# An FFT convolution with a gated unit, forward and backward: spectra kept as separate real and imaginary tiles of two channel blocks, and the step back from them as two 64-row TensorE tiles

## The chip, the cores and the metric

The kernel runs on one NeuronCore of a Trainium2 chip. The metric is the device time of one execution, in microseconds (us). Before the change it is 535.45 us, the median of three runs (534.1 to 536.3).

## What is computed

Forward and all gradients of one block: a layer norm, a long convolution done with an FFT over the sequence (length S = 2048, padded to 4096, D = 512 channels), a gated unit of width F = 1376, and their product added to the input. Inputs and outputs are bfloat16.

```python
def _A_ref(q, k, v, shift_k, ssm_k, ssm_D):
    k_shift = sum of 4 shifted copies of k, each times a column of shift_k
    kv = k_shift * v
    kv_f = rfft(pad(kv, 2 * S)); kf_f = rfft(pad(ssm_k, 2 * S))
    y = irfft(kv_f * kf_f)[:S] + kv * ssm_D
    return q * y

def _B_ref(x, w_gate, w_up, w_down):
    g, u = x @ w_gate, x @ w_up
    return (sigmoid(g) * u) @ w_down

xn = layernorm(A_q)
out = A_q + _A_ref(xn, A_k, A_v, ...) * silu(_B_ref(xn, ...))
# returned: out, and the gradients of A_q, A_k, A_v, A_shift_k, A_ssm_k, A_ssm_D,
# B_w_gate, B_w_up, B_w_down for a given grad_out
```

## The kernel before

**The order.** The kernel does not issue instructions as it is written. Python generators ("streams") yield after each piece of work; `run_streams` takes the next piece from the stream that is furthest behind its share, a start and an end written beside each stream. Every operation goes into a record (`Rec.add`), with the operations it depends on. `Rec.order` then lays all of them out with a cost for each (`cost`, `dcost`) and a model of free PSUM banks, and `emit` (line 505) issues them in that order, so every instruction of the profile has line 505. Copies out of PSUM (`evac`) go to ScalarE or VectorE, as the layout decides. Each engine and each DMA queue then works in the order given.

**PSUM.** There are eight banks. `KINDS` names the slots: `mm2` is a pair of banks for 1024 f32 columns, `acc` (banks 4 and 5) and `tr` (6 and 7) single ones. In the forward stage `mm2` may use all four pairs; from the middle stage on `ps_mm` uses `mm2c`, two pairs.

**Stages.** Forward (`strF`, `strK`, `strV`, `strX` together): the gated unit; the spectrum of the filter; the product of shifted k and v; its spectrum, the product of spectra, and the way back to `y2A`. Middle (`stepB`, with the first pieces of `dW` and `frontC`): gradients through the gated unit. Back (`dW`, `frontC`, `backC`): the weights' gradients, whose operands come through DMA transposes on SP's queue; the spectrum of the gradient; and two ways back, one for the gradient of kv and one for that of the filter.

**The transform of 128 channels** (one group `cg` of four) has three steps. `step1`: 128 matmuls of 128 columns, each with 32 output partitions, four beside each other in the array (column tiles). `flip`: a transpose on VectorE for each block `qq`, a quarter of a group. `step3` (line 881): a matmul with the constant `BD`, 128 by 128, two of 512 columns for a block. Its result has the real part of the spectrum in partitions 0 to 63 and the imaginary part in 64 to 127. Back from a spectrum: `inv3` (line 888) with the spectrum as weights and a constant as moving operand, 8 times 2 matmuls of 128 columns for a block, the two of a pair summing in PSUM; then `inv1`.

**The product of two spectra** needs real with imaginary parts, which lie in other partitions. So `swap` (line 903) makes a second copy with the halves exchanged, by two VectorE copies of 64 partitions: of the filter's spectrum in `strK` (`KF`, `Ks`) and of the gradient's in `frontC` (`Xc`, `Xs`). VectorE multiplies twice per product, and the two results, with their signs in the constants `RS1`, `RS2`, `RC1`, `RC2`, are summed by `inv3`'s pair of matmuls. `strX` has one product for each block, `backC` two (line 1258). 16 blocks are worked through in each.

**KK_d**, in HBM, keeps both forward spectra of each block: `strK` and `strX` store them through POOL's queue (256 KB each), and `ld_KK` loads both of a block (512 KB) on SP's queue into one of three buffers; load n + 3 is recorded after the last `inv3` of block n (line 1267).

Of the kernel before, what the change touches and what calls it, by code (L numbers as in the profile page):

```python
# [16 lines left out]
P = 128  # L17
# [12 lines left out]
NKF = 3  # L30
# [112 lines left out]
class PTile:  # L143

    def __init__(self, kind):
        self.kind = kind
        self.bank = None
        self.left = 0
        self.last = 0.0

# [5 lines left out]
class Op:  # L156
    __slots__ = ("n", "alts", "deps", "succ", "wait", "ready", "dma", "tiles", "done", "fin", "eng", "soft")
# [12 lines left out]
class Rec:  # L170
# [5 lines left out]
    KINDS = {"mm2": [(0, 1), (2, 3), (4, 5), (6, 7)], "mm2c": [(0, 1), (2, 3)], "mm1": [(0,), (1,), (2,), (3,)],  # L176
             "acc": [(4,), (5,)], "tr": [(6,), (7,)]}

    def __init__(self, nc, tc, slab, psum):
        self.nc, self.tc, self.psum = nc, tc, psum  # L180
        self.slab_name = slab.name
        self.ops = []
        self.lastw, self.readers = {}, {}
        self.cache = {}
        self.narrow = False
        for e in self.ENGS:
            setattr(self, e, EngRec(self, e))
# [48 lines left out]
    def add(self, alts):  # L236
# [37 lines left out]
        op.dma = "dma" in meth  # L274
        self.ops.append(op)
# [7 lines left out]

    def cost(self, alt):
# [67 lines left out]
    def order(self):  # L352
# [3 lines left out]
        for op in ops:  # L356
            for v in op.tiles:
                group.setdefault(id(v), []).append(op)
# [44 lines left out]
        while ndone < len(ops):  # L403
            best = None
            for e in self.ENGS:
# [3 lines left out]
                if now[e]:  # L409
                    c = (free[e], now[e][0], e, 0)  # L410
                elif soon[e]:
                    c = (soon[e][0][0], soon[e][0][1], e, 0)
# [13 lines left out]
            if shared:  # L426
                either.remove(op)
            else:
                heapq.heappop(now[e] if now[e] else soon[e])
            q = 1 if shared and e == "vector" else 0  # L430
            new = [v for v in op.tiles if v.bank is None]
            if new:
                got = slot(new[0].kind)
                if got is None:
                    blocked[new[0].kind].append(op)
                    continue
                if got[0] > t:
                    op.ready = got[0]
                    push(op)
                    continue  # L440
                new[0].bank = got[1][0]
                for b in got[1]:
                    owner[b] = new[0]
            alt = op.alts[q]
# [90 lines left out]
class Consts:  # L535
# [27 lines left out]
    def small(self, negpi, TB, I32, after):  # L563
# [33 lines left out]
        an = tmp([5, 128], i32)  # L597
        nc.gpsimd.tensor_scalar(an[:, 0], pr[:, 0], pcf[:, 0:1], None, ALU.add)
        nc.gpsimd.tensor_scalar(an[:, 2], pr[:, 1], pcf[:, 0:1], pcf[:, 0:1], ALU.add, ALU.add)
        nc.gpsimd.tensor_scalar(an[:, 1], an[:, 2], 4.0, None, ALU.add)  # L600
        nc.gpsimd.tensor_scalar(an[:, 3], pr[:, 1], 4.0, None, ALU.add)
        nc.gpsimd.tensor_copy(an[:, 4], pr[:, 1])
        nc.vector.tensor_single_scalar(an, an, 15, ALU.bitwise_and)
        tri = tmp([5, 128], f32)
# [6 lines left out]
        nc.vector.tensor_tensor(TB[:, 1:5], tri[:, 1:5], mask[:, 1:2].to_broadcast([P, 4, 128]), ALU.mult)  # L611
# [11 lines left out]
def kernel_impl(ctx, tc, A_q, A_k, A_v, A_shift_k, A_ssm_k, A_ssm_D, B_x, B_w_gate, B_w_up, B_w_down,  # L623
# [8 lines left out]
    KK_d = dram.tile([NG, 4, 2, P, 1024], bf16, name="KK_d")  # L632
# [13 lines left out]
    def ps_mm(shape, dt=f32, name=None):  # L646
        return nc.ps(PS["mm"], shape, dt)
# [9 lines left out]
    TB = Ring(ar, [5, 128]).ap  # L657
    BD, RC2, RS1, RC1, RS2 = (TB[:, q] for q in (0, 1, 2, 4, 3))
# [187 lines left out]
    Ks_r, KF_r = Ring(ar, [1024], n=NKF), Ring(ar, [1024], n=NKF)  # L846
# [3 lines left out]
    Xc_r = Ring(ar, [1024], n=2)  # L850
# [26 lines left out]
    def step3(Qf, dst):  # L877
        ps = ps_mm([1024], name="ps_x")
        for h in range(2):
            nc.tensor.matmul(ps[:, h * 512:(h + 1) * 512], BD, Qf[:, 2 * h:2 * h + 2].rearrange("p a (k b) -> p a b k", b=2),  # L880
                             start=True, stop=True)
        nc.evac(dst, ps, 1024)

    def inv3(parts, qq, Bg):
        ps = ps_mm([8, NJ, 8], name="ps_b")
        for g in range(8):
            for n, (Y, Rt) in enumerate(parts):
                nc.tensor.matmul(ps[:, g].rearrange("p j x -> p (j x)"), Y[:, g * 128:(g + 1) * 128], Rt,
                                 start=(n == 0), stop=(n == len(parts) - 1))
        nc.evac(Bg[:, :, 8 * qq:8 * qq + 8].rearrange("p j g e c -> p g j (e c)"), ps[:], 1024)  # L890
# [12 lines left out]
    def swap(dst, src):  # L903
        nc.vector.tensor_copy(dst[0:64], src[64:128])
        nc.vector.tensor_copy(dst[64:128], src[0:64])
# [11 lines left out]
    def strK():  # L917
        for cg in range(NG):
# [15 lines left out]
            for qq in range(4):  # L934
                while stA["nX"] + NKF <= 4 * cg + qq:
                    yield 0
                Qf, KF, Ks = QfK_r.next(), KF_r.next(), Ks_r.next()
                flip(Qg, qq, Qf)
                yield 1024
                step3(Qf, KF)  # L940
                swap(Ks, KF)
                nc.gpsimd.dma_start(KK_d[cg, qq, 0], KF)
                stA["K", 4 * cg + qq] = (KF, Ks)
                yield 1024
# [30 lines left out]
    def strX():  # L975
        yield from gen_ci()
        for cg in range(NG):
            while ("QgV", cg) not in stA or ("K", 4 * cg) not in stA:
                yield 0
            Qg = stA.pop(("QgV", cg))  # L980
            Bg = Bg_r.next()
            xs = {}
            for qq in range(5):
                if qq < 4:
                    Qf, Xc = QfV_r.next(), Xc_r.next()
                    flip(Qg, qq, Qf)
                    if qq == 3:
                        flags.add(("flV", cg))
                    yield 1024
                    step3(Qf, Xc)  # L990
                    nc.gpsimd.dma_start(KK_d[cg, qq, 1], Xc)
                    xs[qq] = Xc
                    yield 1024
                if qq > 0:
                    n = 4 * cg + qq - 1
                    while ("K", n) not in stA:
                        yield 0
                    KF, Ks = stA.pop(("K", n))
                    Xc = xs.pop(qq - 1)
# [3 lines left out]
                    stA["nX"] = n + 1  # L1003
                    yield 2048
# [9 lines left out]
    for r in (KT_r, KC_r, kh_r, vg_r, acc_r, term_r, QgK_r, QgV_r, QfK_r, QfV_r, KF_r, Ks_r, Bg_r, Xc_r):  # L1014
        r.free()
# [193 lines left out]
    def ld_KK(n):  # L1209
        if n < 16:  # L1210
            KK = KK_r.next()
            nc.sync.dma_start(KK[:, 0], KK_d[n // 4, n % 4].rearrange("t p x -> p t x"))
            stC["KK", n] = KK

    def frontC():
        for cg in range(NG):
# [4 lines left out]
            for qq in range(4):  # L1221
                n = 4 * cg + qq
                while stC["nY"] + NXC <= n:
                    yield 0
                Qf = Qf_r.next()
                flip(Qg, qq, Qf)
                if qq == 3:
                    flags.add(("fl3", cg))
                yield 1024
                Xc, Xs = Xc_r.next(), Xs_r.next()  # L1230
                step3(Qf, Xc)
                swap(Xs, Xc)
                stC["Y", n] = (Xc, Xs)
                yield 1024
# [13 lines left out]
    def backC():  # L1248
        for cg in range(NG):
            c0, c1 = cg * GW, (cg + 1) * GW  # L1250
            B1, B2 = B1_r.next(), B2_r.next()
            for qq in range(4):
                n = cg * 4 + qq
                while ("Y", n) not in stC:
                    yield 0
                Xc, Xs = stC.pop(("Y", n))
                KK = stC.pop(("KK", n))
                for t in range(2):
# [9 lines left out]
                yield 2048  # L1268
# [75 lines left out]
    Xc_r, Xs_r = Ring(ar, [1024], n=NXC), Ring(ar, [1024], n=NXC)  # L1344
# [4 lines left out]
    KK_r = Ring(ar, [2, 2, 1024], n=3)  # L1349
# [13 lines left out]
    for n in range(3):  # L1363
        ld_KK(n)
    dw, fr = live
    live = run_streams([(dw[0], dw[1] - dw[4], 0.05, 1.0), (fr[0], fr[1] - fr[4], -0.1, 0.65),
                        (gated(backC(), "back"), 4 * 32768, -0.05, 0.66)], until=lambda: "back" in flags)
    for r in (KK_r, Qg_r, B2_r):
        r.free()
# [64 lines left out]
```

## Time and profile before

| | |
|---|---|
| runs of the kernel | 534.1, 535.45, 536.3 us |
| profiled execution, its own time | 537.1 us |
| span of the profile | 535.3 us |
| mean granted TensorE clock | 0.991 |
| HBM read, written | 47.74 MB, 51.55 MB |

The span is what the profile's views divide up; the execution's time has some 1.8 us around it. A view by lines says little here, because all instructions come from one line; groups by shape, by tile name or by stretch of time tell the parts of the kernel apart. "slab" is the one SBUF allocation that holds all tiles, "psum" all of PSUM. In shapes such as 128*32, the first number is the rows and the second the columns of the array in use.

### The profile page before, as it was taken

Reading aid. Unit: us, or ns where it says so; the run is one execution under the profiler, and the core shown is the slowest. Engines: PE = TensorE matmul, PEld = TensorE weight load, DVE = VectorE, ACT = ScalarE, POOL = GpSimd, SP = SyncE. Lnnn points to the kernel's source line nnn. Section 1 sums busy time; section 2 is a strip of 40 time slices with the busy share of each in tenths; the row PEclk is TensorE's granted clock in tenths of the full one; section 3 lists DMA queues with packets and bytes.
Section 4 is the critical chain, followed back from the end, with each engine's and each line's share of the span. In section 5 each row is a group of like instructions: output and inputs, shape, how many; then the busy total and the mean of one; then the engine's idle time right before and its main releaser. Section 6 shows DMA issues by size and latency. Waiting matters only on the chain.

```text
span 535.3 us, 12895 instructions
## 1 busy us (share of the span) xinstructions
PE 492.8 (92%) x5441; PEld 327.0 (61%) x5441; DVE 397.4 (74%) x622; ACT 302.8 (57%) x360; POOL 68.3 (13%) x118
## 2 busy tenths in 40 slices
PE   3998599999899999899988999999999998799995
PEld 2867376767667776566564564445756655665643
DVE  7779779999996857988888684349688485564924
ACT  5976485989698755353453342338756656434421
POOL 7631222322423210000000000000000000000000
PEclk9999899999999999999999999999999999899998
DMA  8964729582626969999999597589889997999983
GB/s 284 275 209 148 244 90 323 195 278 99 240 107 256 202 247 268 242 299 379 351 312 325 176 295 208 140 145 288 221 193 198 259 280 132 255 218 199 175 213 109
DMA packets 187140, 121.46 MB, mean 227 GB/s; under 512 B 116362, under 2 KB 169034, under 8 KB 187083
## 3 DMA queue, kind: packets, MB, share of 16 engines
q1 hardware_dynamic: 178760, 91.41, 68.2%
q0 software_dynamic: 7360, 28.45, 14.1%
q8 instruction: 42, 0.69, 0.5%
q10 hardware_dynamic: 962, 0.79, 0.5%
q14 instruction: 16, 0.12, 0.1%
HBM read 47.74 MB, written 51.55 MB: 185 GB/s over the span
## 4 chain that ended last, share of the span: by engine, by line
PE 54%; DVE 6%; DMA 3%; ACT 2%; SPq 1%; issue 1%; DVEq 0%; ACTq 0%
PE psum L505 54%; DVE slab L505 6%; ACT slab L505 2%; DMA slab<-KK_d 2%; SPq L505 1%; DMA out_dram<-slab 1%; DMA slab<-slab 1%; DVEq L505 0%; ACTq L505 0%
## 5 line engine op out<-in xcount | busy, mean ns | idle before, releaser
L505 PE MATMUL psum<-slab 128*128 128x128 bf16 (+5 forms) x5441 | 492.8, 266 | 36.3 <-DVE slab L505 19.6
L505 PEld LDWEIGHTS <-slab 128*128 128x128 bf16 (+2 forms) x5441 | 327.0, 99 | 201.8 <-issue 30.6
L505 DVE TENSOR_TENSOR slab<-slab 128x1024 bf16<-128x1024 bf16 (+4 forms) x312 | 246.6, 835 | 44.0 <-ACT slab L505 16.8
L505 ACT CAST slab<-psum 128x1024 bf16<-128x1024 f32 (+4 forms) x225 | 200.5, 931 | 128.6 <-PE psum L505 115.9
L505 ACT ACTIVATE slab<-psum 128x1024 bf16<-128x1024 f32 (+2 forms) x56 | 48.3, 884 | 74.0 <-PE psum L505 73.1
L505 DVE SCALAR_TENSOR_TENSOR slab<-slab 128x512 f32<-128x512 bf16 (+1 forms) x56 | 26.9, 480 | 38.9 <-ACT slab L505 36.2
L505 DVE TENSOR_TENSOR slab<-psum,slab 128x1024 bf16<-128x1024 f32 (+2 forms) x36 | 37.8, 1053 | 14.4 <-ACT slab L505 13.2
L505 DVE STREAM_TRANSPOSE slab<-slab 128x512 int32<-128x512 int32 x48 | 32.6, 698 | 13.8 <-PE psum L505 8.8
L505 POOL MEMSET slab<- 1x384 bf16 (+2 forms) x13 | 4.5, 353 | 259.5 <-PE psum L505 257.2
L505 ACT ACTIVATE slab<-slab 128x512 f32<-128x512 bf16 (+3 forms) x33 | 28.8, 891 | 7.4 <-DVE slab L505 7.1
L505 DVE COPY slab<-slab 64x1024 bf16<-64x1024 bf16 (+1 forms) x68 | 28.6, 420 | 3.8 <-ACT slab L505 2.3
L505 ACT COPY slab<-psum 128x1024 bf16<-128x1024 bf16 (+1 forms) x24 | 23.3, 986 | 13.0 <-PE psum L505 13.0
L505 POOL DMA_DIRECT2D KK_d<-slab x32 | 18.0, 562 | 75.1 <-ACT slab L505 73.6
L505 DVE CAST slab<-psum 128x1024 bf16<-128x1024 f32 (+1 forms) x8 | 9.3, 1158 | 8.9 <-PE psum L505 5.5
L505 POOL DMA_DIRECT2D hS_d<-slab x8 | 8.8, 1097 | 22.0 <-DVE slab L505 21.8
L505 POOL TENSOR_TENSOR slab<-slab 128x2 f32<-128x2 f32 (+2 forms) x13 | 9.9, 769 | 7.4 <-DVE slab L505 5.8
L505 DVE BATCH_NORM_STATS2 slab<-slab 128x6 f32<-128x512 bf16 x16 | 10.5, 680 | 0.4 <-DMA slab<-in_A_q_dram 0.4
L505 ACT ACT_TABLE_LOAD x6 | 7.7, 1283 | 3.9 <-issue 3.8
L505 DVE TENSOR_SCALAR slab<-slab 128x2 f32<-128x2 f32 (+5 forms) x23 | 8.1, 390 | 0.2
L505 DVE COPY slab<-psum 128x1024 bf16<-128x1024 bf16 x6 | 4.0, 687 | 3.7 <-PE psum L505 3.7
L505 POOL TENSOR_SCALAR slab<-slab 128x128 int32<-128x128 f32 (+4 forms) x8 | 5.4, 680 | 1.2 <-DVE slab L505 0.8
L505 POOL DMA_DIRECT2D slab<-in_A_q_dram x6 | 3.7, 618 | 9.1 <-ACT slab L505 7.3
(17 smaller groups left out, 28.4 us busy)
## 6 DMA issues: line engine op xcount, KB each, us to landing
KK_d<-slab POOLq DMA_DIRECT2D x32, 256.0 KB, 3.0
slab<-KK_d SPq DMA_DIRECT2D x16, 512.0 KB, 5.0
hS_d<-slab POOLq DMA_DIRECT2D x8, 704.0 KB, 7.4
duS_d<-slab SPq DMA_DIRECT2D x8, 704.0 KB, 5.8
dgS_d<-slab SPq DMA_DIRECT2D x8, 704.0 KB, 7.3
zS_d<-slab POOLq DMA_DIRECT2D x6, 768.0 KB, 5.7
slab<-zS_d SPq DMA_DIRECT2D x6, 768.0 KB, 7.1
sF_d<-slab POOLq DMA_DIRECT2D x6, 704.0 KB, 5.5
```

What stands on the lines that cost most here:

```text
L505: getattr(getattr(self.nc, eng), meth)(*[place(v) for v in a], **{x: place(v) for x, v in k.items()})
```

## The change

Two blocks are worked on together, as a pair `pp`. `step3` writes two tiles for them: c = 0 has the real parts of both blocks (64 partitions each) and c = 1 the imaginary parts, so that the parts that are multiplied with each other stand in the same partitions. It does so with matmuls of 32 output partitions each, four beside each other. The swaps go. The product of two spectra is now two multiplications of 2048 columns (one factor broadcast over both halves), a subtraction and an addition of 1024 columns on VectorE. `inv3` takes one block from partitions 0 to 63 and the other from 64 to 127, as matmuls with 64 rows, with each block writing its own PSUM bank.

```diff
-    BD, RC2, RS1, RC1, RS2 = (TB[:, q] for q in (0, 1, 2, 4, 3))
+    BD, RI, RR = (TB[:, q] for q in range(3))
...
-    def step3(Qf, dst):
-        ps = ps_mm([1024], name="ps_x")
+    def step3(Qfs, dst):
+        ps = None
+        for c in range(2):
+            ps = ps_mm([1024], name="ps_x", lead=ps)
+            for h in range(2):
+                for q in range(4):
+                    nc.tensor.matmul(ps[32 * q:32 * q + 32, h * 512:(h + 1) * 512],
+                                     BD[:, 64 * c + 32 * (q % 2):64 * c + 32 * (q % 2) + 32],
+                                     Qfs[q // 2][:, 2 * h:2 * h + 2].rearrange("p a (k b) -> p a b k", b=2), start=True, stop=True)
+            nc.evac(dst[:, c], ps, 1024)
+
+    def inv3(Y, pp, Bg):
+        Bv = Bg.rearrange("p j (q h g) e c -> p q h j (g e c)", q=4, h=2)
+        ps = None
         for h in range(2):
-            nc.tensor.matmul(ps[:, h * 512:(h + 1) * 512], BD, Qf[:, 2 * h:2 * h + 2].rearrange("p a (k b) -> p a b k", b=2),
-                             start=True, stop=True)
-        nc.evac(dst, ps, 1024)
-
-    def inv3(parts, qq, Bg):
-        ps = ps_mm([8, NJ, 8], name="ps_b")
-        for g in range(8):
-            for n, (Y, Rt) in enumerate(parts):
-                nc.tensor.matmul(ps[:, g].rearrange("p j x -> p (j x)"), Y[:, g * 128:(g + 1) * 128], Rt,
-                                 start=(n == 0), stop=(n == len(parts) - 1))
-        nc.evac(Bg[:, :, 8 * qq:8 * qq + 8].rearrange("p j g e c -> p g j (e c)"), ps[:], 1024)
+            ps = ps_mm([2, NJ, 32], name="ps_b", lead=ps)
+            for gl in range(4):
+                g = 4 * h + gl
+                for c, R in enumerate((RR, RI)):
+                    for q in range(2):
+                        qs = slice(64 * q, 64 * q + 64)
+                        nc.tensor.matmul(ps[:, q, :, 8 * gl:8 * gl + 8], Y[qs, c, g * 128:(g + 1) * 128],
+                                         R[qs].rearrange("p (j x) -> p j x", x=8), start=(c == 0), stop=(c == 1))
+            nc.evac(Bv[:, 2 * pp:2 * pp + 2, h], ps[:], 1024)
+        yield 2048
...
-                    nc.vector.tensor_tensor(KF, Xc, KF, ALU.mult)
-                    nc.vector.tensor_tensor(Ks, Xc, Ks, ALU.mult)
-                    inv3([(KF, RS1), (Ks, RS2)], qq - 1, Bg)
+                KP, Y = stA.pop(("K", n)), T_r.next()
+                nc.vector.tensor_tensor(Y, both(KP[:, 0:1]), XP, ALU.mult)
+                nc.vector.tensor_tensor(KP, both(KP[:, 1:2]), XP, ALU.mult)
+                nc.vector.tensor_tensor(Y[:, 0], Y[:, 0], KP[:, 1], ALU.subtract)
+                nc.vector.tensor_tensor(Y[:, 1], Y[:, 1], KP[:, 0], ALU.add)
+                yield from inv3(Y, pp, Bg)
...
-                    nc.vector.tensor_tensor(KK[:, 1, t], Xs, KK[:, 0, t], ALU.mult)
-                    nc.vector.tensor_tensor(KK[:, 0, t], Xc, KK[:, 0, t], ALU.mult)
+                    T2 = T_r.next()
+                    Ts.append(T2)
+                    nc.vector.tensor_tensor(T2, both(KK[:, t, 0:1]), YP, ALU.mult)
+                    nc.vector.tensor_tensor(KK[:, t], both(KK[:, t, 1:2]), YP, ALU.mult)
+                    nc.vector.tensor_tensor(T2[:, 0], T2[:, 0], KK[:, t, 1], ALU.add)
+                    nc.vector.tensor_tensor(T2[:, 1], T2[:, 1], KK[:, t, 0], ALU.subtract)
                 stC["nY"] = n + 1
-                if qq == 2:
+                if pp == 1:
                     ld_bwd(cg)
-                inv3([(KK[:, 0, 0], RC1), (KK[:, 1, 0], RC2)], qq, B1)
-                yield 2048
-                inv3([(KK[:, 0, 1], RC1), (KK[:, 1, 1], RC2)], qq, B2)
-                ld_KK(n + 3)
-                yield 2048
+                ld_KK(n + 2)
+                yield from inv3(Ts[0], pp, B1)
+                yield from inv3(Ts[1], pp, B2)
```

The record's layout knows the new shapes and takes both PSUM slots of a `step3` or an `inv3` at once (`lead`, `mate`):

```diff
-            if out.ap.ap[0][1] == 32:
-                c /= 4
-            if (out.ap.ap[0][1] == 32) != self.narrow:
-                self.narrow = not self.narrow
+            mode = self.mode(alt)
+            c *= min(mode) / P
+            if mode != self.narrow:
+                self.narrow = mode
                 c += 0.095
...
+                more = new[0].mate
+                if more is not None:
+                    for b in got[1]:
+                        owner[b] = new[0]
+                    also = slot(more.kind)
+                    for b in got[1]:
+                        owner[b] = None
+                    if also is None:
+                        blocked[new[0].kind].append(op)
+                        continue
+                    got = (max(got[0], also[0]), got[1])
```

It also gains a way to prefer matmuls of the shape that is set (`WIN`, `WINN`, `HOLD`); with the three at 0 it never applies. `KK_d` holds pairs: stores of 512 KB in place of 256, loads of 1 MB in place of 512 KB, two load buffers in place of three, and load n + 2 recorded ahead of `inv3`. In the back stage `ps_mm` uses `mm2d`, which adds banks 6 and 7 to `mm2c`. The streams' shares are new:

```diff
-    live = run_streams([(strF(), NU * 34816, 0.0, 1.06), (strK(), 4 * 14336, 0.0, 0.8), (strV(), 4 * 12288, 0.07, 0.82),
-                        (gated(strX(), "X"), 4 * 20480 + 4096, 0.2, 1.0)], until=lambda: "X" in flags)
+    live = run_streams([(strF(), NU * 34816, 0, 1.06), (strK(), 4 * 14336, 0, 0.9), (strV(), 4 * 12288, 0.07, 0.72),
+                        (gated(strX(), "X"), 4 * 16384 + 4096, 0.2, 1)], until=lambda: "X" in flags)
...
-    live = run_streams(live + [(dW(), 35 * 8192, 0.92, 1.35), (frontC(), 4 * 12288, 1.25, 1.4)], until=lambda: "B" in flags)
+    live = run_streams(live + [(dW(), 35 * 8192, 0.92, 1.35), (frontC(), 4 * 12288, 1.05, 1.45)], until=lambda: "B" in flags)
...
-    live = run_streams([(dw[0], dw[1] - dw[4], 0.05, 1.0), (fr[0], fr[1] - fr[4], -0.1, 0.65),
-                        (gated(backC(), "back"), 4 * 32768, -0.05, 0.66)], until=lambda: "back" in flags)
+    live = run_streams([(dw[0], dw[1] - dw[4], 0.05, 0.95), (fr[0], fr[1] - fr[4], -0.1, 0.55),
+                        (gated(backC(), "back"), 4 * 24576, -0.05, 0.96)], until=lambda: "back" in flags)
```

More of the change, by code (lines that the diff above doesn't have):

```diff
@@ L29 @@
 GQ = GW // 4
-NKF = 3
+NKP = 2
+WIN = 0
+WINN = 0
+HOLD = 0.0
 NXC = 2
@@ L156 @@
 class Op:
[L157 removed]
+    __slots__ = ("n", "alts", "deps", "succ", "wait", "ready", "dma", "tiles", "done", "fin", "eng", "soft", "mode")
 class EngRec:
@@ L409, in order @@
                 if now[e]:
+                    if e == "tensor" and ops[now[e][0]].mode != self.narrow:
+                        lim = now[e][0] + (WIN if self.narrow == (P, P) else WINN)
+                        n0 = min((n for n in now[e] if ops[n].mode == self.narrow), default=lim)
+                        if n0 < lim:
+                            now[e].remove(n0)
+                            now[e].sort()
+                            now[e].insert(0, n0)
+                        else:
+                            s = min((x for x in soon[e] if x[0] < free[e] + HOLD and x[1] < lim and ops[x[1]].mode == self.narrow), default=None)
+                            if s is not None:
+                                soon[e].remove(s)
+                                heapq.heapify(soon[e])
+                                free[e] = s[0]
+                                now[e].insert(0, s[1])
                     c = (free[e], now[e][0], e, 0)
@@ L443, in order @@
                     owner[b] = new[0]
+                if more is not None:
+                    more.bank = also[1][0]
+                    for b in also[1]:
+                        owner[b] = more
             alt = op.alts[q]
@@ L631, in kernel_impl @@
     ksh_d = dram.tile([NG, P, NJ * GW], bf16, name="ksh_d")
-    KK_d = dram.tile([NG, 4, 2, P, 1024], bf16, name="KK_d")
+    KK_d = dram.tile([NG, 2, 2, P, 2048], bf16, name="KK_d")
     hS_d = dram.tile([NU, FP, 256], bf16, name="hS_d")
@@ L644, in kernel_impl, with ps_mm @@
     PS = {}
-    def ps_mm(shape, dt=f32, name=None):
-        return nc.ps(PS["mm"], shape, dt)
+    def ps_mm(shape, dt=f32, name=None, lead=None):
+        pt = nc.ps(PS["mm"], shape, dt)
+        if lead is not None:
+            lead.tile.mate, pt.tile.lead = pt.tile, lead.tile
+        return pt
     def ps_acc(shape, dt=f32, name=None):
@@ L901, in inv1, with both @@
             yield 2048
-    def swap(dst, src):
-        nc.vector.tensor_copy(dst[0:64], src[64:128])
-        nc.vector.tensor_copy(dst[64:128], src[0:64])
+    def both(x):
+        return x.to_broadcast([P, 2, 1024])
     def strF():
@@ L933, in strK @@
             yield from step1(lambda j: KC[:, j, :], Qg)
-            for qq in range(4):
-                while stA["nX"] + NKF <= 4 * cg + qq:
+            for pp in range(2):
+                while stA["nX"] + NKP <= 2 * cg + pp:
                     yield 0
[L937 to L944, printed above, removed]
+                Qfs = [QfK_r.next(), QfK_r.next()]
+                for q in range(2):
+                    flip(Qg, 2 * pp + q, Qfs[q])
+                    yield 1024
+                KP = KP_r.next()
+                step3(Qfs, KP)
+                nc.gpsimd.dma_start(KK_d[cg, pp, 0], KP.rearrange("p c x -> p (c x)"))
+                stA["K", 2 * cg + pp] = KP
+                yield 2048
     def strV():
@@ L1220, in frontC @@
             yield from step1(lambda j: y2A[:, j, cg * GW:(cg + 1) * GW], Qg)
-            for qq in range(4):
-                n = 4 * cg + qq
+            for pp in range(2):
+                n = 2 * cg + pp
                 while stC["nY"] + NXC <= n:
                     yield 0
-                Qf = Qf_r.next()
-                flip(Qg, qq, Qf)
-                if qq == 3:
-                    flags.add(("fl3", cg))
[L1229 to L1234, printed above, removed]
+                Qfs = [Qf_r.next(), Qf_r.next()]
+                for q in range(2):
+                    flip(Qg, 2 * pp + q, Qfs[q])
+                    yield 1024
+                if pp == 1:
+                    flags.add(("fl3", cg))
+                YP = YP_r.next()
+                step3(Qfs, YP)
+                stC["Y", n] = YP
+                yield 2048
     def ld_bwd(cg):
```

99 lines of the change are left out of this document (55 added, 44 removed).

## The prediction

> **What bounds the kernel now.** I read the page first: busy shares, busy tenths, the chain of waits.
>
> ```profile
> span 535.3 us, 12895 instructions
> PE 492.8 (92%) x5441; PEld 327.0 (61%) x5441; DVE 397.4 (74%) x622; ACT 302.8 (57%) x360; POOL 68.3 (13%) x118
> ...
> PE   3998599999899999899988999999999998799995
> ...
> DVE  7779779999996857988888684349688485564924
> ...
> DMA  8964729582626969999999597589889997999983
> ...
> PE 54%; DVE 6%; DMA 3%; ACT 2%; SPq 1%; issue 1%; DVEq 0%; ACTq 0%
> ```
>
> TensorE is the bound: 92% busy, and 54% of the span in the chain, whose first piece that could be followed starts at 166 us. An average over stages hides differences, so the second view is the busy time by stage. The cuts follow from the tile view of `KK_d`, the spectra in HBM: stored in the forward stage, loaded in the last one.
>
> ```profile
> L505 POOL DMA_DIRECT2D KK_d<-slab x32: 539/542/767, 36.0 to 191.4; - x32
> L505 SPq DMA_DIRECT2D slab<-KK_d x16: 373/392/2045, 326.8 to 491.0; - x16
> ```
>
> ```profile
> core 0: us, PE busy (x) PEld busy (x) DVE busy (x) ACT busy (x) POOL busy (x), PEclk, DMA share, GB/s
> 0.00:205.00 205.00, 183.46 (x2482) 137.01 (x2483) 172.62 (x267) 153.20 (x164) 65.63 (x113) 0.99 0.67 214
> 205.00:327.00 122.00, 114.71 (x762) 71.11 (x760) 98.63 (x159) 48.60 (x70) 1.49 (x2) 1.00 0.98 289
> 327.00:510.00 183.00, 175.55 (x2094) 108.54 (x2093) 118.56 (x190) 96.84 (x119) 1.22 (x3) 0.99 0.96 208
> ```
>
> ```profile
> 80.00:120.00 40.00, 38.30 (x560) 27.54 (x558) 39.06 (x55) 30.84 (x34) 11.98 (x21) 1.00 0.80 267
> 120.00:160.00 40.00, 36.41 (x549) 27.39 (x548) 37.29 (x60) 34.22 (x39) 12.29 (x17) 1.00 0.42 149
> ```
>
> Forward (0 to 205): between 80 and 160 VectorE is busy 39.1 and 37.3 of 40 us and TensorE 38.3 and 36.4, so the two share the bound there. Middle (205 to 327): TensorE, with the DMA engines at 0.98. Back stage (327 to 510): TensorE 175.6 of 183 us, VectorE 118.6, DMA 0.96: TensorE's time is the end's time, and DMA is close behind it.
>
> The third view is the groups of instructions by shape.
>
> ```profile
> L505 PE MATMUL psum<-slab 128*128 128x512 bf16 x1056 | 248.0, 381 | 6.0 <-DVE slab L505 5.6 <-ACT slab L505 0.3
> L505 PE MATMUL psum<-slab 128*128 128x128 bf16 x1384 | 95.7, 221 | 11.4 <-DVE slab L505 9.6 <-ACT slab L505 1.7
> L505 PE MATMUL psum<-slab 128*32 128x128 bf16 x1792 | 32.5, 222 | 6.9 <-issue 3.7 <-DVE slab L505 3.0
> L505 ACT CAST slab<-psum 128x1024 bf16<-128x1024 f32 x177 | 174.0, 1022 | 91.4 <-PE psum L505 80.3 <-DMA out_dram<-slab 3.9 <-DVE slab L505 2.7
> L505 DVE TENSOR_TENSOR slab<-slab 128x1024 bf16<-128x1024 bf16 x176 | 114.4, 687 | 15.5 <-DMA slab<-KK_d 11.7 <-ACT slab L505 1.9 <-PE psum L505 0.4
> L505 DVE TENSOR_TENSOR slab<-slab 128x2048 bf16<-128x2048 bf16 x92 | 111.4, 1216 | 27.9 <-ACT slab L505 14.9 <-DMA slab<-slab 12.1
> L505 DVE COPY slab<-slab 64x1024 bf16<-64x1024 bf16 x64 | 28.0, 437 | 3.8 <-ACT slab L505 2.3
> ```
>
> The 128x128 and the 128*32 matmuls have the same mean (221 and 222 ns), because these are latencies of overlapping instructions. What a matmul costs TensorE is the distance from its start to the next start, and that takes the fourth view, the timeline of TensorE in short windows (start, length, then the count).
>
> ```profile
> 368.16 1.05 PE L505 MATMUL psum<-slab 128*128 128x128 bf16 x16 [0.30 <-ACT slab L505]
> 385.80 0.38 PE L505 MATMUL psum<-slab 128*128 128x512 bf16 x1
> 386.02 0.38 PE L505 MATMUL psum<-slab 128*128 128x512 bf16 x1
> 386.33 0.29 PE L505 MATMUL psum<-slab 128*32 128x128 bf16 x8
> 387.01 0.40 PE L505 MATMUL psum<-slab 128*32 128x128 bf16 x16
> 387.34 0.39 PE L505 MATMUL psum<-slab 128*128 128x512 bf16 x1
> ```
>
> The first row is one `inv3` call: 16 matmuls in 1.05 us, less the last one's 0.22, over 15 distances: **55 ns each**. The next five are a run of 64 narrow matmuls (four column tiles of 32) inside a run of full ones. It starts at 386.33 and ends at 387.01 + 0.40 = 387.41; less 0.22 that is 0.86 us, or 13.4 ns each, so four tiles together take what one full 128-column matmul takes. Its edges show **a change of tile shape**: full matmuls start 386.02 - 385.80 = 0.22 apart, but the first narrow one comes 0.31 after the last full one, 0.09 more; on the way out the full one starts 0.15 after the last narrow start (387.19), of which some 0.055 is streaming, again 0.09.
>
> **The change part by part.**
>
> *`inv3`, two 64-row tiles.* Before there are 16 forward and 32 backward calls of 16 matmuls: 768, or 768 x 55 ns = 42.2 us. After there are still 768 of 128 columns, but each uses 64 rows, and neighbours use opposite halves of the array and separate PSUM banks. If two run together, as four column tiles do in the rows above, a matmul costs 28 ns: -21.1 us, of which -7.0 forward (256) and -14.1 back (512). No row shows a 64-row tile, so this is bounded: 28 ns at best, 55 ns (no gain) if each load and matmul still goes through alone. I take 28, since the narrow rows, the nearest, show full overlap with one weight load per matmul.
>
> The Trainium skill's page "TensorE: Matmul & The Clock Gate", section "LDWEIGHTS (loading the stationary operand)", speaks against this: a load's time goes by its columns (columns / 1.2 ns) and fewer rows do not shorten it. By that figure a 128-column load is 107 ns, 768 of them one after another are 82 us, and the time would be about 586 us, an estimate; the 55 ns rows, each with a 128-column load, already contradict it as a floor. The skill's "TensorEngine Tiling (Array Packing)", section "Key Properties", says that different tiles load and multiply in parallel, which gives the 28 ns; no run here shows either for row tiles.
>
> *Changes of tile shape.* `step3` becomes narrow and `inv3` 64-row; both were full. Counted along TensorE's instruction order, the shape changes 66 times before (40 forward, 0 middle, 26 back) and 190 times after (94, 4, 92): +124. At 0.093 us this is **+11.5 us**: +5.0 forward, +0.4 middle, +6.1 back. The price is from narrow edges; 66 of the new edges touch a 64-row run. Bounds for those: nothing (-6.1) and a full drain, the 0.22 of a 128x128 row (+8.4). I take 0.093, the nearest row.
>
> *`step3`, four 32-column tiles.* 96 full matmuls of 512 columns, 0.22 us apart (the pace of the 512-column rows at 385.80 and 386.02), become 384 narrow ones; four at a time that is again 96 x 0.22 = 21 us. The narrow run shows four together at 128 columns; longer streams have fewer starts to hide, so zero, at most a us either way.
>
> *VectorE.* The 64 half-height copies (`swap`) go. Per pair of blocks, forward: 4 products x 0.687 + 4 copies x 0.437 = 4.50 us become 2 x 1.216 + 2 x 0.687 = 3.81; eight pairs, -5.5 us. Back: 8 x 0.687 + 4 x 0.437 = 7.24 become 4 x 1.216 + 4 x 0.687 = 7.61; +2.9 us. The 1.216 row is 92 instructions, of which 32 already multiply by a broadcast operand, so I take the broadcast as free; the dear bound is two short products, 1.374, or +7.6 us over the 48 long ones. The back stage's +2.9 lies beside TensorE's `dW` matmuls (118.6 of 183 us busy); without that cover it costs 2.9.
>
> *Evacuations* keep number and size (1024 columns, 1.02 us on ScalarE), but each `step3` and `inv3` now asks for two PSUM slots at once, and two copies follow each other.
>
> *DMA.* 32 stores of 256 KB become 16 of 512 KB on POOL, which is 13% busy: nothing. 16 loads of 512 KB on SP become 8 of 1 MB, with two buffers (four blocks) in place of three. Loads are where the back stage waits now, in the chain and on SP's queue:
>
> ```profile
> 436.86 7.59 SPq L505 DMA_TRANSPOSE slab<-dgS_d  x5
> 444.55 0.53 SPq L505 DMA_DIRECT2D out_dram<-slab  x1
> 445.20 4.32 SPq L505 DMA_TRANSPOSE slab<-dgS_d  x3
> ```
>
> ```profile
> 451.55 4.27 DMA slab<-KK_d
> 490.95 4.53 DMA slab<-KK_d
> ```
>
> The load issued at 451.55 stands behind eight transposes of about 1.5 us each. SP keeps these transposes in the new order, and queued behind a late load are the next group's loads. After the change a load is issued once the products are done, no longer after `inv3` has read them, but it carries twice the data. I leave the 8.8 us as they are; bounds -8.8 and +8.8 (the same two waits, twice the bytes).
>
> *The sum.* Forward: TensorE -7.0 + 5.0 = -2.0, VectorE -5.5; as they share the bound, -3. Middle +0.4. Back -14.1 + 6.1 = -8.0, and +0.6 for VectorE where the chain sits on it. Together -10.0: span 535.3 to 525.3. The profiled execution took 537.1 us, 1.65 above the median of the runs, 535.45; off the median it gives **525.5 us**, -1.9%.
>
> **The rivals.**
>
> *Row tiles do not overlap* (slower). Each 64-row matmul keeps its 55 ns because its 128-column load is not shortened by having half the rows; then only the changes of shape are left: 535.45 + 11.5 = **547 us**. For it: the count of loads and their columns stay. Against it: four narrow loads and matmuls fit in the time of one. It decides from 40 ns a matmul on: there the 768 x 15 ns saved only pay for the 11.5 us.
>
> *DMA holds the back stage.* With a share of 0.96 and the transposes in SP's order, TensorE's 8.0 us turn into waits for transposes and loads: 535.45 - 3 + 0.4 = **533 us**. For it: 0.96 and the 8.8 us above. Against it: those are two waits in 183 us.
>
> *The load waits go.* Eight loads in place of 16, issued earlier: 525.5 - 8.8 = **517 us**. Against it: the same transposes ahead.
>
> *PSUM pairs starve TensorE.* A pair of `inv3` slots is computed in 0.9 us and copied out in two of 1.02 us. If half of the 24 paired calls leave TensorE idle for one copy, +12: **538 us**. Against it: `dW` has accumulators of its own and fills such holes. The Trainium skill's "TensorEngine Tiling (Array Packing)", section "PSUM Bottleneck", names this rule: tiling speeds up the array but not the copies.
>
> **How the numbers follow.** The forecast has 0.55 (its own range 519 to 534, from the price of the 64-row edges), no overlap 0.22, load waits gone 0.12, DMA 0.07, PSUM 0.04. Half a per cent, about what a measurement of this kernel tells from no change, is 2.7 us: faster below 532.8, slower above 538.1. Forecast and load waits are faster (0.67), DMA and PSUM within (0.11), no overlap slower (0.22). The range runs from the third rival's 517 to the first one's 547, since the price of a 64-row tile is open between 28 and 55 ns.
>
> **What would show it.** Two `inv3` matmuls per 55 ns in short TensorE windows, 0.09 us more at each change of shape, four 512-column narrow matmuls per 0.22 us, no 64-row copies and 128x2048 products near 1.22 us on VectorE; TensorE's back stage some 8 us shorter. The prediction is wrong if 64-row matmuls start 50 ns or more apart, if a change to 64 rows costs 0.2 us or more, or if the chain of the back stage moves from TensorE to DMA.

## The result, and the profile after

| | before | changed |
|---|---|---|
| time, median | 535.45 us (534.1 to 536.3, 3 runs) | **520.75 us** (518.4 to 522.5, 4 runs) |
| ratio | | 0.9726, 95% interval 0.9671 to 0.9781 |
| span of the profile | 535.3 us | 518.5 us |
| the changed kernel once more, later | 535.19 us (17 runs) | 522.49 us (6 runs), 0.9756, 0.9705 to 0.9808 |

Faster by 2.7% in the first measurement and by 2.4% in the second; 1.9% was forecast. Executions of a kernel that stand more than 1.5% above its fastest are left out of every number here: one of the kernel before (542.6 us), one of "full rows, new order" (546.1) and three of the four of "one share changed" (547.5 to 556.5).

The page of the changed kernel (busy time and share by engine; busy tenths in 40 slices; the chain's shares, which here run from the start of the span and not from 166 us on, so that 61% is not to be held against the 54% of before):

```profile
span 518.5 us, 13287 instructions
...
PE 477.3 (92%) x5670; PEld 300.4 (58%) x5729; DVE 397.8 (77%) x561; ACT 293.9 (57%) x355; POOL 57.4 (11%) x100
...
PE   3999878999999999799999999999999998999984
...
PE 61%; DVE 17%; DMA 9%; ACT 5%; issue 4%; POOL 1%; SPq 1%; DVEq 0%; POOLq 0%; ACTq 0%
```

VectorE's busy time did not change (397.4 to 397.8 us), TensorE's fell. 59 matmul records are missing in this profile (5670 against 5729 weight loads; all are of the full 512-column shape, 901 of 960), so TensorE's busy time is not compared further. The groups by shape show what came in place of what (count, then busy time, mean):

```profile
L552 DVE TENSOR_TENSOR slab<-slab 128x2048 bf16<-128x2048 bf16 x140 | 168.5, 1216 | 28.9 <-DMA slab<-slab 7.9 <-PE psum L552 6.8 <-ACT slab L552 6.4
...
L552 PE MATMUL psum<-slab 64*128 64x128 bf16 x768 | 28.0, 220 | 2.7 <-DVE slab L552 2.7
L552 PE MATMUL psum<-slab 128*32 128x512 bf16 x384 | 27.3, 391 | 0.0
```

The product with a broadcast factor takes 1.216 us, as the long products did before. The 768 matmuls of 64 rows and the 384 narrow ones of 512 columns are there. How dense the 64-row ones stand is read from TensorE's timeline in three short windows (start, length, count):

```profile
383.49 0.38 PE L552 MATMUL psum<-slab 128*128 128x512 bf16 x1
383.80 1.07 PE L552 MATMUL psum<-slab 64*128 64x128 bf16 x32
384.80 0.39 PE L552 MATMUL psum<-slab 128*128 128x512 bf16 x1
```

32 matmuls in 1.07 us, less 0.22 for the last, over 31 distances: **27 ns each**, half of the 55 of before. The run starts 0.31 us after the full matmul ahead of it, 0.09 more than the 0.22 of a full one. The last starts at 384.65; the next full one comes 0.15 later, 0.09 more than a pair needs. A change to 64 rows costs what a change to narrow columns does. The narrow matmuls of 512 columns, in `step3`, start in fours: over the whole profile a four follows the one before it after 0.225 to 0.239 us, 0.23 in the mean, where a full matmul of 512 columns takes 0.216.

**TensorE's work** can now be added up for each kernel: count times start-to-start distance in these profiles (0.2158 us for 512 columns, 0.149 for 352, 0.109 for 256, 0.0558 for 128; a quarter of it for narrow, half for 64-row matmuls), and 0.093 for each change of shape. Before: 469.1 + 66 x 0.093 = 475.3 us. Changed: 447.7 + 190 x 0.093 = 465.4 us. That is -9.9 us (-8.5 with 0.23 us for each four of `step3`), and the span fell by 16.8 (by 13.7 in the second profile, 521.6). So what is left of the span, called idle time of TensorE below, fell too, from 60.0 to 53.1 and 56.2 us. The experiments ask where that comes from, and what the row tiles alone are worth.

The tile view of `KK_d` of the changed kernel has the one wait that is gone for certain:

```profile
L552 SPq DMA_DIRECT2D slab<-KK_d x8: 371/414/532, 334.2 to 449.6; - x8
...
who waited for it (us, times):
```

Nobody waits for a load any more; before, the chain had 8.8 us of it. In its place the chain's pieces in the back stage show halo copies (`slab<-slab`, the three rows that `backC` moves between partitions). Each halo is two copies, of 84 KB and of 11.2 KB, and the chain's pieces are the small second ones:

```profile
395.34 7.19 DMA slab<-slab
...
432.13 6.59 DMA slab<-slab
...
500.68 4.35 DMA slab<-slab
```

On SP's queue the second copy does not follow the first: loads, stores and transposes are issued between them, and here it comes 14.4 us later (11.3, 15.3 and 2.0 us for the other three).

```profile
380.97 0.97 SPq L552 DMA_DIRECT2D slab<-slab  x1
395.34 0.96 SPq L552 DMA_DIRECT2D slab<-slab  x1
```

### The profile page after: what moved, and what is told of

It reads as the page before. It is cut to its first block, busy times and chain, and to the rows that moved or that the text cites. A ratio compares the mean times of both kernels' runs of the same rounds, so it can differ in the third digit from the quotient of the medians.

```text
span 518.5 us, 13287 instructions
## 1 busy us (share of the span) xinstructions
PE 477.3 (92%) x5670; PEld 300.4 (58%) x5729; DVE 397.8 (77%) x561; ACT 293.9 (57%) x355; POOL 57.4 (11%) x100
## 4 chain that ended last, share of the span: by engine, by line
PE 61%; DVE 17%; DMA 9%; ACT 5%; issue 4%; POOL 1%; SPq 1%; DVEq 0%; POOLq 0%; ACTq 0%
PE psum L552 61%; DVE slab L552 17%; ACT slab L552 5%; DMA slab<-slab 3%; DMA slab<-in_A_k_dram 2%; POOL slab L552 1%; DMA slab<-sF_d 1%; DMA slab<-in_A_q_dram 1%; SPq L552 1%; DMA out_dram<-slab 1%; ACT L552 0%; DVEq L552 0%; ACTq L552 0%; POOLq L552 0%; POOLq L1481 0%
## 5 line engine op out<-in xcount | busy, mean ns | idle before, releaser
L552 PE MATMUL psum<-slab 128*32 128x128 bf16 (+7 forms) x5670 | 477.3, 270 | 33.7 <-DVE slab L552 12.1
L552 PEld LDWEIGHTS <-slab 128*128 128x128 bf16 (+3 forms) x5729 | 300.4, 98 | 210.3 <-issue 52.1
L552 DVE TENSOR_TENSOR slab<-slab 128x2048 bf16<-128x2048 bf16 (+4 forms) x312 | 272.4, 914 | 33.9 <-PE psum L552 7.9
L552 ACT CAST slab<-psum 128x1024 bf16<-128x1024 f32 (+4 forms) x219 | 192.0, 930 | 118.2 <-PE psum L552 96.9
L552 ACT COPY slab<-psum 128x1024 bf16<-128x1024 bf16 (+1 forms) x27 | 25.9, 991 | 4.2 <-PE psum L552 4.0
L552 DVE CAST slab<-psum 128x1024 bf16<-128x1024 f32 (+1 forms) x14 | 16.5, 1185 | 13.7 <-PE psum L552 8.1
L552 POOL DMA_DIRECT2D KK_d<-slab x16 | 8.7, 545 | 40.4 <-ACT slab L552 33.8
L552 DVE BATCH_NORM_STATS2 slab<-slab 128x6 f32<-128x512 bf16 x16 | 10.6, 676 | 0.7 <-DMA slab<-in_A_q_dram 0.7
L552 POOL DMA_DIRECT2D slab<-in_grad_out_dram x6 | 3.3, 554 | 19.5 <-DVE slab L552 19.5
L552 POOL IOTA slab<- 128x128 f32 (+4 forms) x10 | 4.5, 478 | 0.4 <-POOLq L1481 0.4
L552 POOL DMA_DIRECT2D sF_d<-slab x6 | 3.4, 567 | 9.8 <-ACT slab L552 9.6
```

What stands on the lines that cost most here:

```text
L552: getattr(getattr(self.nc, eng), meth)(*[place(v) for v in a], **{x: place(v) for x, v in k.items()})
```

## The experiments

All times are medians; "before" ran beside each but the first (534.9 to 535.2 us). Work is added up as above, idle is the span less work.

| run | time | ratio to before, 95% | span | shape changes | work | idle |
|---|---|---|---|---|---|---|
| before | 535.45 | | 535.3 | 66 | 475.3 | 60.0 |
| changed | 520.75 | 0.967 to 0.978 | 518.5 | 190 | 465.4 | 53.1 |
| changed again | 522.49 | 0.971 to 0.981 | 521.6 | 190 | 465.4 | 56.2 |
| full rows, same order | 526.85 | 0.979 to 0.990 | 524.3 | 126 | 480.9 | 43.4 |
| full rows, new order | 536.07 | 0.999 to 1.006 | 533.6 | 110 | 479.4 | 54.2 |
| old shares | 534.53 | 0.997 to 1.002 | 533.3 | 201 | 466.4 | 66.9 |
| one share changed | 532.97 (one run) | | 530.9 | 172 | 463.7 | 67.2 |
| idle copies, new order | 529.36 | 0.987 to 0.994 | 531.1 | 186 | 465.0 | 66.1 |
| idle copies, same order | 521.34 | 0.972 to 0.978 | 521.5 | 190 | 465.4 | 56.1 |
| two PSUM slots | 522.1 | 0.970 to 0.980 | 521.3 | 182 | 464.6 | 56.7 |
| before, loads on POOL | 529.25 | 0.983 to 0.995 | 530.3 | 64 | 475.1 | 55.2 |
| changed, halo on POOL | 517.74, 515.91 | 0.960 to 0.973, 0.961 to 0.971 | 516.0, 517.7 | 187 | 465.1 | 50.9, 52.6 |
| changed, halo and loads on POOL | 522.97 | 0.973 to 0.981 | 521.3 | 187 | 465.1 | 56.2 |

Idle is not all waiting. In the profile with the old shares TensorE pauses for 6.0 us, and the stretch in which it starts again has a granted clock of 0.50:

```profile
474.50:481.30 6.80, 4.37 (x38) 2.21 (x39) 1.23 (x1) 1.04 (x2) 0.00 (x0) 0.50 1.04 317
```

Such stretches, where TensorE has work in them, last 3.4 or 6.8 us; each of those in the profiles of before, changed, old shares, one share and idle copies with a new order comes a few us after one or two pauses of 1.1 to 6 us, and within them full 512-column matmuls start 0.427 us apart in place of 0.216. Half of TensorE's busy time in them, an estimate of what they cost, is 3.0 us before, 1.7 and 3.4 us in the two profiles of the changed kernel, 5.6 with the old shares, 5.3 with one share changed and 7.9 with idle copies in a new order. So a pause of TensorE costs more than its own length, and some 2 to 4 of the 11 to 14 us by which idle time is larger with the old shares are slow matmuls.

**Full rows, same order.** The row tiles alone are undone: `RZ` holds the constants, zero in the other block's half, and the order is laid out as if the matmuls still had 64 rows.

```diff
-                        nc.tensor.matmul(ps[:, q, :, 8 * gl:8 * gl + 8], Y[qs, c, g * 128:(g + 1) * 128],
-                                         R[qs].rearrange("p (j x) -> p j x", x=8), start=(c == 0), stop=(c == 1))
+                        rec.half = True
+                        nc.tensor.matmul(ps[:, q, :, 8 * gl:8 * gl + 8], Y[:, c, g * 128:(g + 1) * 128],
+                                         RZ[:, c, q].rearrange("p (j x) -> p j x", x=8), start=(c == 0), stop=(c == 1))
+                        rec.half = False
```

> The changed kernel in the same instruction order, but inv3's 768 matmuls use all 128 rows: the moving constant is padded with zeros in the half that does not belong to the block. Result unchanged. Theory 'row tiles': a matmul goes back from 28 to 55 ns (+21 us), the 66 edges of 64-row runs go (-6 us): 520.75 + 15 = about 536 us, forward part perhaps half hidden behind VectorE, so 532 to 537, and 16 inv3 matmuls spaced 55 ns. Rival 'the gain came from VectorE, the load waits or the new order': 515 to 522 us.

526.85 us, 6.1 above the changed kernel's first measurement and 4.4 above its second, and so between the theories. The 32 matmuls that filled 383.80 to 384.87 above do stand 56 ns apart here (30 of them: 1.84 us less 0.22, over 29 distances), and TensorE's work grew by 15.5 us; but idle time fell by 9.7 and 12.8. The timeline and the chain from 327 us on in this run:

```profile
389.79 1.84 PE L561 MATMUL psum<-slab 128*128 128x128 bf16 x30
```

```profile
by line: PE psum L561 92.9%; issue 0.9%; ACT slab L561 0.2%
```

The same stretch in the changed kernel:

```profile
by line: PE psum L552 67.9%; DMA slab<-slab 8.9%; DVE slab L552 7.2%; SPq L552 2.6%; DMA out_dram<-slab 2.4%; issue 1.6%; ACT slab L552 0.9%; DVEq L552 0.0%; ACTq L552 0.0%
```

With full rows nothing but TensorE sets the back stage; with row tiles it has run ahead of the transfers and waits for them. In this order, then, 4 to 6 of the 15.5 us arrive.

**Full rows, new order.** The same instructions, laid out with their real cost (without the line `rec.half = True`).

> The changed kernel with full-row inv3 matmuls (zero-padded constants, result unchanged), this time laid out anew with their real cost; shape changes fall from 190 to 110. TensorE's work is about 14 us above the changed kernel's. Theory 'the order is fitted to the row tiles, and TensorE's work counts in full once it is laid out anew': 532 to 540 us, no better than the kernel before. Rival 'the full-row matmuls cost the 6 us of the run in the old order, whatever the order': 524 to 529 us.

536.07 us, not to be told from the kernel before. The first theory holds for the time, with a reservation: the shares were not sought anew for this version. Between the two runs with full rows the instructions are the same and the work differs by 1.5 us the other way, yet the times differ by 9 us. Order alone does that.

**Old shares.** The shares of the kernel before in the changed one (the three `run_streams` lines).

> The changed kernel with the streams' shares of the kernel before (strK to 0.8, strV to 0.82, frontC 1.25 to 1.4, dW to 1.0, frontC to 0.65, backC to 0.66 in the back stage). TensorE's work stays within 1 us (201 shape changes for 190). Theory 'the part of the gain that is not TensorE's work, some 7 us of idle time, comes from the new shares': 525 to 530 us. Rival 'it comes from the products, the loads and the pairs themselves': 519 to 523 us.

534.53 us, more than either theory had: the whole gain is gone, with TensorE's work only 1 us higher. Idle time is 66.9 us. The largest hole, 6.0 us, is seen in the chain as the wait for a store:

```profile
468.40 7.59 DMA out_dram<-slab
```

`dW` waits at 476.6 for a buffer whose store to the outputs is on its way. The loss lies mainly behind the forward stage. The last matmul of the last forward `inv1` starts at 201.0 us, where the two profiles of the changed kernel have 197.9 and 200.8; from there to the first load of the spectra it takes 140.7 us in place of 136.3 and 137.1, and from that load to the end 191.6 in place of 184.3 and 183.7.

**One share.** `strK` ends at 0.85 in place of 0.9.

> The changed kernel with one share changed: strK ends at 0.85 in place of 0.9. All instructions are the same, TensorE's work within 2 us (172 shape changes for 190, some 1.7 us less). Theory 'several us of the result hang on how the order happens to fall, which the shares decide': 526 to 535 us, all of it idle time of TensorE. Rival 'the loss with the old shares was those particular shares': 519 to 523 us.

533.0 us in the one execution used, with the lowest work of all and 67.2 us idle, as the first theory has it. One execution gives no interval; as far as it goes, a step of 0.05 in one share costs nearly what the old shares cost.

**Idle copies, new order and same order.** 32 half-height VectorE copies into a tile that nobody reads, in `strK`; in the second run the layout counts them as free, so all else keeps its place.

```diff
+                for c in range(2):
+                    nc.vector.tensor_copy(idle_r.ap[0:64], KP[64:128, c, 0:960])
+                    nc.vector.tensor_copy(idle_r.ap[64:128], KP[0:64, c, 0:960])
```

> The changed kernel with 32 half-height VectorE copies of 960 columns put back in the forward stage (strK), into a tile that nobody reads; some 0.42 us each, +13.4 us of VectorE, laid out anew. Theory 'VectorE sets the forward stage': +10 to +13 us, 531 to 534 us. Rival 'TensorE sets it': +0 to +3 us, 521 to 524 us.

> The changed kernel with the same 32 idle half-height VectorE copies in the forward stage, but with the order of all other instructions on every engine kept as in the changed kernel (the layout takes the copies as free). Theory 'VectorE shares the forward bound': the last inv1 of the forward stage, at 197.9 us now, moves by 7 to 13 us, and the time with it, 528 to 534 us. Rival 'VectorE has slack there, and the loss in the run with a new order was the new order': moves by 0 to 4 us, 521 to 525 us.

The copies take 13.0 us of VectorE. With a new order 529.36 us, between the theories, but the last matmul of the last forward `inv1` starts at 201.2; most of the loss came later, where nothing was added. In the same order it starts at 202.9, and the time is 521.34, the rival's range. Six profiles that share the forward order of the changed kernel, without the copies, have that place at 197.9 to 201.0. So it moved by 1.9 to 5.0 us, 0.15 to 0.4 us for each us of VectorE: VectorE holds the forward stage at most in part, and at the end no loss can be told. The first run's answer was mostly its order.

**Two PSUM slots** in the back stage (without `PS["mm"] = "mm2d"`).

> The changed kernel without the third PSUM slot in the back stage (mm2c in place of mm2d). Each step3 and inv3 then takes all of the slots for matmuls while it runs and is copied out. Theory 'pairs of slots starve TensorE': back stage 5 to 12 us longer, 526 to 533 us. Rival 'dW fills the holes': 520 to 523 us.

522.1 us: no loss that can be told. Pairs of slots do not starve TensorE.

**Before, loads on POOL's queue.**

```diff
-            nc.sync.dma_start(KK[:, 0], KK_d[n // 4, n % 4].rearrange("t p x -> p t x"))
+            nc.gpsimd.dma_start(KK[:, 0], KK_d[n // 4, n % 4].rearrange("t p x -> p t x"))
```

> The kernel before with the 16 KK_d loads issued on POOL's queue, so that they no longer stand behind the DMA transposes on SP; laid out anew. Theory 'SP's order made the two load waits': the 8.8 us of DMA slab<-KK_d in the chain go, 527 to 531 us. Rival 'another wait takes their place': 534 to 537 us, with slab<-slab or out_dram<-slab in the chain instead.

529.25 us, 5.9 less than the kernel before: the load waits were SP's order, and were worth most of their 8.8 us. TensorE's weight loads keep the order of the kernel before up to 452.8 us; that the new order behind it has a share is not ruled out. Another wait came up in the chain:

```profile
457.30 4.97 DMA slab<-in_A_k_dram
```

**Changed, halo copies on POOL's queue, alone (twice) and with the loads.**

```diff
-            nc.sync.dma_start(dks[0:112, NJ:NJ + 3, :], dks[1:113, 0:3, :])
-            nc.sync.dma_start(dks[112:127, NJ:NJ + 3, :], dks[113:128, 0:3, :])
+            nc.gpsimd.dma_start(dks[0:112, NJ:NJ + 3, :], dks[1:113, 0:3, :])
+            nc.gpsimd.dma_start(dks[112:127, NJ:NJ + 3, :], dks[113:128, 0:3, :])
```

> The changed kernel with the eight halo copies (slab<-slab, inside the back stage) on POOL's queue instead of SP's; laid out anew. Theory 'what is left of the back stage's waits is SP's order': the chain's 18 us of DMA slab<-slab shrink to some 10 and the time falls to 511 to 517 us. Rival 'TensorE has other work at those places': 519 to 522 us.

> The changed kernel itself, to stand beside the next run on the same chip: 520 to 522 us.

> The run with the eight halo copies on POOL's queue once more, beside the changed kernel: 2 to 4 us below it if the first result (517.7) was the copies, within 1 us if it was the chip.

> The changed kernel with both the halo copies and the eight KK_d loads on POOL's queue. Theory 'SP's order is what keeps TensorE's saving in the back stage from arriving': below the run with the halo copies alone (517.7), 511 to 516 us. Rival 'the loads are early enough already; nobody waits for them in the changed kernel': 516 to 520 us.

Alone: 517.74 us, between theory and rival, and 515.91; the changed kernel beside the second took 522.49, so 6.6 us less there and 3.0 between the two first measurements. Of the second pair all six runs (514.9 to 520.5) lie below five of the changed kernel's six (521.4 to 524.8; the sixth took 519.0). This is the fastest version here. The two copies of a halo now follow each other within 0.5 to 1.5 us:

```profile
382.62 0.57 POOL L552 DMA_DIRECT2D slab<-slab  x1 [36.79 <-DVE slab L552]
384.10 0.53 POOL L552 DMA_DIRECT2D slab<-slab  x1
```

Of the chain's 18.1 us of halo copies 9.9 are left in the first profile and none in the second. TensorE's order is that of the changed kernel up to some 393 us and another one behind it, so the queue and the order after it are not told apart in these two runs. With the loads as well, 522.97, above what both theory and rival had: TensorE waited 6 us for a transpose, in front of its weight load at 360.6,

```profile
360.60 0.13 PEld L552 LDWEIGHTS <-slab 128*128 128x128 bf16 x2 [6.40 <-DMA slab<-hS_d]
```

a wait that the changed kernel does not have. TensorE's order is the same as with the halo copies alone, to the last weight load. What differs there is the second load of the spectra, which on POOL's queue no longer stands behind SP's transposes. It and the piece of the chain that holds TensorE:

```profile
349.34 0.72 POOL L552 DMA_DIRECT2D slab<-KK_d  x1 [3.71 <-DMA out_dram<-slab]
```

```profile
349.17 11.39 DMA slab<-hS_d
```

Issued at 349.34 us, and not at 356.35 as with the halo copies alone, the load runs beside the transposes. It lands after 11.2 us in place of 5.3, and the transpose that TensorE waits for takes until 360.6. Moving a transfer that nobody waited for made another one late; this rests on one profile.

## Why the prediction was right

The sign, the range (517 to 547) and the mechanism on TensorE held; the size was forecast at 10.0 us and measured at 14.7 and, later, 12.7. The first measurement, 520.75, lies nearer to the third rival's 517 than to the 525.5; the second, 522.49, the other way.

- *Row tiles, 55 to 28 ns.* Right: 27 ns, for two matmuls in different halves with a 128-column load each. The rival without overlap (547) is out. The Trainium skill's "TensorEngine Tiling (Array Packing)", section "Key Properties", says that different tiles load and multiply in parallel, and the 27 ns agree with it for 64-row tiles. The 107 ns for a 128-column load, an estimate by the rule of the Trainium skill's "TensorE: Matmul & The Clock Gate", section "LDWEIGHTS (loading the stationary operand)", did not bound these 27 ns.
- *Changes of shape, 124 at 0.093 us.* Right, at 64-row edges too (0.09 in and out); neither bound for them came into play.
- *`step3`.* Four narrow matmuls of 512 columns start 3 to 4 ns apart, often a little more, and the next four 0.23 us after the first four, where 0.22 was assumed: for 96 fours that is 1.4 us, a little beyond the us that was allowed.
- *VectorE.* The long product is 1.216 us, and its busy time as a whole did not change. That the forward stage gains 3 us, between TensorE's 2.0 and VectorE's 5.5, is borne out roughly: the last matmul of the last forward `inv1` starts 6.2 us earlier in the first profile and 3.4 in the second. How the gain divides between the two engines is not shown; by the idle copies a us of VectorE is worth 0.15 to 0.4 there.
- *The term that was mis-sized: "I leave the 8.8 us as they are".* From the end of the forward stage to the end of the span the profiles fell by 10.6 and 10.4 us where 7.0 were forecast. The waits for the loads went, as the third rival had it; but halo copies and output stores, late in the same queue, came up instead, so that of the 8.8 us a net 3.5 came on top of the forecast. That the loads' place in SP's queue was their cause is shown by the kernel before with the loads on POOL; how the 3.5 divide between larger, earlier loads and the new order as a whole was not separated.
- *What the sum took for granted.* It added TensorE's savings as if idle time stood still. It does not: at fixed order 15.5 us of work changed the time by 4 to 6, and idle time went from 53 to 67 us between orders of the same instructions. That the sum came out near is in part luck: the order was laid out anew, with shares that suit it, and with the old shares the same instructions give nothing. The prediction named the shares nowhere, and this was a rival that it lacked. The kernel before was not run with the new shares or any others, so how much of the 12.7 to 14.7 us shares alone would have given it is open.
- *PSUM pairs* (538) and *DMA holds the back stage* (533): the first is out, since the run with fewer slots lost nothing; the second is half true, since with row tiles the back stage does wait for transfers, though it kept the gain, and TensorE still has most of its chain (74.4% before, 67.9% after).

## What to carry to other kernels

Add up a change on the bounding engine as count times start-to-start distance, with the changes of mode in it; the sum of TensorE's terms was right to some 1 us (-9.6 forecast, -8.5 to -9.9 counted). Then ask what the order does with it: where a planner lays out the instructions anew, a shift of its weights moved this kernel by 10 to 14 us (the smallest shift on one execution), so one version at one setting measures the setting too, and an edit is best also tried with the order of all else held fixed. Where an engine runs ahead of the transfers, look at the queue in which they stand behind one another: moving eight small copies to a queue with little on it, with the order that came of it, gave another 3 to 7 us here. And a pause of TensorE is best counted with the stretch of half clock behind it.

## What was not expected of the hardware

Two 64-row matmuls start 3 to 4 ns apart and the next pair 52 ns later, at 128 columns, with a weight load for each. Four narrow ones of 512 columns take 0.23 us together, 0.014 more than a full one. A change between full and 64-row shape costs 0.09 us, as one between full and 32-column shape does. Pauses of TensorE of 1 to 6 us are followed by stretches of 3.4 or 6.8 us at a granted clock of 0.50. A halo copy of only 11.2 KB on SP took 4.4 to 7.2 us from its issue to its landing in the chain's three pieces (the four of 84 KB: 3.0 in the median), and stood up to 15 us behind the copy that it belongs with.
